# Moving eighteen more exp chunks from ScalarE to VectorE in a fused attention and MLP kernel, with the cost of small jobs reckoned anew

## The chip, the cores and the metric

The kernel runs on one core of one Trainium2 chip. The time is device time in microseconds (us) of one execution; the median of several runs is given, and for every experiment the ratio to the kernel before, timed in the same rounds on the same chip. A ratio is the mean time of one kernel's fast runs over that of the other's of the same rounds, so it is not quite the ratio of the medians that are quoted. Runs of the kernel before lay between 971.1 and 973.6 us in the various rounds; so where two experiments are compared across rounds, their ratios are compared, as a share of 971.5 us.

## The reference, cut to what matters

```python
kv_pool = kv.reshape(B, H//4, 4, W//4, 4, C).mean(axis=(2, 4))     # B 4, C 128, 768 keys per batch
k = v = kv_pool.reshape(B, -1, C) @ w_sr
a = softmax(q @ k.T / sqrt(C))                                     # 49152 queries in all
x = a @ v
h = x @ w_in                                                       # d_ff 2048
out = (h * sigmoid(1.702 * h)) @ w_out
```

The inputs and the output are float32; the kernel computes its matmuls in bf16.

## The kernel before

A *chunk* is 128 keys (or 128 of the d_ff features) by 512 queries. There are 96 groups of 512 queries; four groups make a supergroup. A group needs 6 exp chunks and 16 Gelu chunks. TensorE computes the scores of three chunks into three banks of PSUM (a "fill"), ScalarE takes exp or Gelu of the three in one instruction into a buffer `ag` of 102 slots, and TensorE later multiplies each slot by the values or by `w_out` (a "drain"). So that ScalarE changes its table only three times, the work runs in four stages: attention of the first half, its MoE (the MLP), attention of the second half, its MoE. I call them attention 0, MoE 0, attention 1 and MoE 1.

VectorE already makes the exp of 24 *early* chunks during MoE 0, with a polynomial of ten instructions:

```python
def early_fill(i, jc):
    ps = acc()
    rhs = qTs[i // 4][:, 0, (i % 4) * G:(i % 4 + 1) * G]
    nc.tensor.matmul(ps, kTs[i // GB][:, jc * 128:(jc + 1) * 128], rhs, start=True, stop=True)
    steps = early_exp(ps, weights(("a", i, jc)))
...
def early_exp(ps, out):
    nc.vector.tensor_scalar(a, ps, scale / LN2, -126.0, MUL, MAX)
    yield 3.5
    nc.vector.tensor_scalar(b, a, 127.0, MAGIC, MIN, ADD)
    yield 2.2
    ...
```

The program is written in a fixed order per engine, and the order comes from a reckoning made while it is written: `now` is TensorE's time and `dve` VectorE's, in units of one 512-column matmul (0.2158 us), and `end` is when each activation would end. A drain is placed between two fills when, by the reckoning, its inputs are ready and the next fill is still in time. Nothing of this reckoning happens on the chip. There, TensorE takes its matmuls in the order written, and waits where an input is late (the section on the result shows a wait of 9.11 us in which the matmuls behind it stand still too).

```python
    FIXED, CHUNK, SWITCH, HANDOVER, EVACUATE, LATE = 0.33, 1.975, 6.0, 1.0, 4.5, 1.0
    COST = {pool_chunk: (2.5, 2.0), key_chunk: (0.7, 2.0), ...}
...
        end.append(begin + FIXED + CHUNK * len(part))
```

The transposed queries of a supergroup, `qT`, are loaded by a DMA from supergroup 4 on (before that TensorE transposes them). The load for supergroup s + 2 is issued when ScalarE's fills reach s.

The softmax here doesn't subtract the row's maximum and nothing guards it: scores larger than these inputs give would overflow.

## Time and profile before

972.39 us (median of 3, 972.28 to 972.58); the profiled execution has a span of 969.7 us.

| | busy us | share of the span |
|---|---|---|
| TensorE matmul (PE) | 946.0 | 98% |
| ScalarE (ACT) | 946.4 | 98% |
| VectorE (DVE) | 344.0 | 35% |
| GpSimd (POOL) | 65.7 | 7% |

In the groups, "x512" is the number of instructions, then come busy time and the mean length of one in ns, then the idle time of the engine just ahead of them and what ended it. TensorE's busy time is no measure of its fullness; the prediction shows how its work was counted in its place. The chain of waits of before is shared by ScalarE and TensorE (the page's part on the chain that ended last, by engine and by line):

```profile
ACT 48%; PE 47%; DMA 3%; DVE 1%; issue 1%; POOL 0%; POOLq 0%
```

### The profile page before, as it was taken

The numbers are of one execution on the slowest core, as the hardware profiler recorded it, in microseconds if no ns is written. First come the engines' busy times: TensorE is split into PE (matmuls) and PEld (weight loads), VectorE is DVE, ScalarE is ACT, GpSimd is POOL, SyncE is SP. The second block draws the span as 40 slices with busy tenths as digits, with TensorE's granted clock in tenths as the row PEclk, the third lists the DMA queues.
The fourth block names the chain that finished last, engine by engine and source line by source line (L and its number), as shares of the span: only waits on it lengthen the run. The fifth ranks groups of instructions, "written<-read, shape, count | busy, mean of one in ns | idle before, by whom it ended". The sixth has DMA issues, their size and how long they took to land.

```text
span 969.7 us, 15127 instructions
## 1 busy us (share of the span) xinstructions
PE 946.0 (98%) x6244; PEld 504.7 (52%) x6359; DVE 344.0 (35%) x734; ACT 946.4 (98%) x705; POOL 65.7 (7%) x113
## 2 busy tenths in 40 slices
PE   7899999999999999999999999999999999999997
PEld 3567777544444444454445777754444444444443
DVE  4444433201477778777602333311111011011010
ACT  4999999999999999999999999999999999999997
POOL 3100100340000232000000000000000000000000
PEclk9999999999999999999999999999999999999999
DMA  9899841999862698224348994652222222222222
GB/s 182 161 201 148 110 96 34 108 147 172 162 130 44 103 149 110 41 34 76 57 81 132 182 174 106 131 120 40 37 44 39 38 44 34 43 34 40 37 33 43
DMA packets 354164, 89.66 MB, mean 92 GB/s; under 512 B 328048, under 2 KB 351728, under 8 KB 353776
## 3 DMA queue, kind: packets, MB, share of 16 engines
q1 hardware_dynamic: 323936, 56.06, 33.7%
q0 software_dynamic: 29104, 32.51, 22.6%
q8 instruction: 49, 0.80, 0.3%
q10 hardware_dynamic: 1056, 0.13, 0.1%
q14 instruction: 19, 0.16, 0.1%
HBM read 52.49 MB, written 45.88 MB: 101 GB/s over the span
## 4 chain that ended last, share of the span: by engine, by line
ACT 48%; PE 47%; DMA 3%; DVE 1%; issue 1%; POOL 0%; POOLq 0%
ACT ag L515 36%; PE banks L513 17%; PE banks L520 17%; ACT ag L336 13%; PE banks L345 6%; PE banks L334 5%; DMA qT<-q_bf 2%; DMA x<-in_q_dram 1%; DVE qT L230 1%; PE banks L382 1%; PE banks L424 0%; PE banks L224 0%; DVE o_sb L528 0%; ACT L515 0%; PE banks L134 0%
## 5 line engine op out<-in xcount | busy, mean ns | idle before, releaser
L515 ACT ACTIVATE ag<-banks 128x1536 bf16<-128x1536 f32 x512 | 690.0, 1543 | 1.6 <-PE banks L513 1.5
L513 PE MATMUL banks<-x,w_in_sb 128*128 128x512 bf16 x1484 | 411.2, 379 | 2.9
L520 PE MATMUL banks<-ag,w_out_sb 128*128 128x512 bf16 x1517 | 410.0, 379 | 1.8 <-ACT ag L515 0.5
L336 ACT ACTIVATE ag<-banks 128x1536 bf16<-128x1536 f32 (+1 forms) x188 | 250.6, 1445 | 12.2 <-PE banks L334 11.7
L520 PEld LDWEIGHTS <-w_out_sb 128*128 128x128 bf16 x1536 | 149.6, 97 | 181.7 <-issue 1.6
L513 PEld LDWEIGHTS <-w_in_sb 128*128 128x128 bf16 x1536 | 147.6, 97 | 176.5 <-issue 20.1
L528 DVE STREAM_TRANSPOSE o_sb<-banks 128x512 f32<-128x512 f32 x96 | 68.7, 716 | 398.8 <-PE banks L520 386.5
L345 PEld LDWEIGHTS <-ag 128*128 128x128 bf16 x2304 | 146.4, 98 | 45.4 <-issue 1.2
L345 PE MATMUL banks<-v,ag 128*128 128x129 bf16 x2304 | 162.9, 220 | 0.4 <-DVE v L158 0.3
L334 PE MATMUL banks<-qT,kT 128*128 128x512 bf16 x508 | 146.9, 379 | 9.3 <-ACT ag L336 4.8
L354 DVE RECIPROCAL rec<-banks 128x3 f32<-128x3 f32 x128 | 23.0, 180 | 132.9 <-PE banks L345 132.7
L409 DVE SCALAR_TENSOR_TENSOR ea<-ea,eb 128x512 f32<-128x512 f32 x96 | 65.9, 687 | 2.8
L334 PEld LDWEIGHTS <-kT 128*128 128x128 bf16 x552 | 47.4, 98 | 36.2 <-issue 4.5
L362 DVE TENSOR_TENSOR x<-banks,rec 128x384 bf16<-128x384 f32 x104 | 57.9, 557 | 3.6
L166 POOL DMA_DIRECT2D kvs<-in_kv_dram x32 | 40.4, 1319 | 15.8 <-DMA kvs<-in_kv_dram 11.6
L449 POOL MEMSET gate_tile<- 1x8 f32 x38 | 4.0, 106 | 461.9 <-DVE gate_tile L448 461.9
L398 DVE TENSOR_SCALAR ea<-banks 128x512 f32<-128x512 f32 x24 | 16.6, 691 | 30.1 <-PE banks L382 30.1
L411 DVE SCALAR_TENSOR_TENSOR ag<-ea,ee 128x512 bf16<-128x512 f32 x24 | 16.5, 686 | 1.0
L404 DVE SCALAR_TENSOR_TENSOR eb<-eb,ea 128x512 f32<-128x512 f32 x24 | 16.5, 688 | 0.7
L362 DVE TENSOR_TENSOR xt<-banks,rec 128x384 bf16<-128x384 f32 x24 | 13.4, 557 | 0.8
L230 DVE COPY qT<-banks 128x512 bf16<-128x512 bf16 x15 | 9.8, 686 | 4.8 <-PE banks L224 4.6
L426 DVE COPY x<-banks 128x768 bf16<-128x768 bf16 x12 | 6.7, 557 | 12.0 <-PE banks L424 11.9
(65 smaller groups left out, 154.5 us busy)
## 6 DMA issues: line engine op xcount, KB each, us to landing
out_dram<-o_sb SPq DMA_DIRECT2D x382, 64.0 KB, 2.0
kvs<-in_kv_dram POOLq DMA_DIRECT2D x32, 384.0 KB, 6.2
q_bf<-in_q_dram POOLq DMA_DIRECT2D x20, 512.0 KB, 7.3
x_bf<-x SPq DMA_DIRECT2D x13, 768.0 KB, 5.7
x<-in_kv_dram POOLq DMA_DIRECT2D x12, 512.0 KB, 12.3
x<-in_q_dram POOLq DMA_DIRECT2D x3, 512.0 KB, 20.6
w_in_sb<-in_moe_w_in_dram POOLq DMA_DIRECT2D x1, 512.0 KB, 5.1
w_out_sb<-in_moe_w_out_dram POOLq DMA_DIRECT2D x1, 512.0 KB, 6.6
```

What stands on the lines that cost most here:

```text
L166: nc.gpsimd.dma_start(out=kv_sums[b][:, i2], in_=kv_p[b, i, w, :, i2], **({"accum_op": ADD} if n else {}))
L230: nc.vector.tensor_copy(dst, src)
L334: nc.tensor.matmul(ps[:, k, :], kTs[i // GB][:, jc * 128:(jc + 1) * 128], rhs, start=True, stop=True)
L336: nc.scalar.activation(place([("a",) + c for c in chunks]), ps, AF.Exp, scale=scale)
L345: nc.tensor.matmul(av_of[u][:, k * (C + 1):(k + 1) * (C + 1)], weights(("a", i, jc))[:, o:o + T], vs[i // GB][:, jc, 0:C + 1], start=(jc = ...
L354: nc.vector.reciprocal(rec, ps[:, :, C])
L362: nc.vector.tensor_tensor(to, ps[:, :, 0:C], rec.unsqueeze(2).broadcast_to([128, TS, C]), MUL)
L409: nc.vector.scalar_tensor_tensor(a, a, COEFFS[k], b, ADD, MUL)
L513: nc.tensor.matmul(ps[:, k, :], w_in_sb[:, fc * 128:(fc + 1) * 128], x[:, g % (4 * XS) * G:(g % (4 * XS) + 1) * G], start=True, stop=True)
L515: nc.scalar.activation(place([("m",) + c for c in chunks]), ps, AF.Gelu_apprx_sigmoid)
L520: nc.tensor.matmul(o_of[g], w_out_sb[:, fc, :], weights(("m", g, fc)), start=(fc == 0), stop=(fc == FCH - 1))
L528: nc.vector.transpose(o_sb, o_of.pop(g))
```

## The change

The intent: ScalarE is full, VectorE is not. So one chunk of every supergroup, the last one, goes to VectorE within both attentions too: supergroups 5 to 11 and 13 to 23, 18 chunks. Their results lie in a ring of three slots, `aside`. A chunk's matmul may be placed when the fills have reached the supergroup before its own. And the small jobs of TensorE and the activation are reckoned at their measured length. The diff, cut to its core:

```diff
+    rolling = [(4 * s + 3, JC - 1) for s in range(NS) if 4 * s > early[-1] or QS < s < XS]
+    aside = agpool.tile([128, K, 512], BF, name="aside")
...
+    def early_fits(p, i, jc):
+        if (i, jc) in rolling:
+            group = seq[p][1][0][0] if seq[p][0] == "a" else ...
+            return (i // GB, jc) in vs and i // 4 - 1 <= group // 4 and len(used) > rolling.index((i, jc)) - K
+        return low and min(slot_of.values()) >= low and (2, JC - 1) in vs
+    def early_waits(t):
+        return any(made.get((t // 4, jc), 1e9 if (t // 4, jc) in early_todo else 0.0) > now for jc in range(JC))
...
-    FIXED, CHUNK, SWITCH, HANDOVER, EVACUATE, LATE = 0.33, 1.975, 6.0, 1.0, 4.5, 1.0
-    COST = {pool_chunk: (2.5, 2.0), key_chunk: (0.7, 2.0), value_chunk: (0.7, 2.0),
-            transpose_q: (1.2, 4.0), early_fill: (1.0, 5.5), key_and_value: (1.0, 3.0),
-            transpose_pooled: (1.5, 3.0), make_k: (1.0, 3.0), make_v: (1.5, 3.0), turn: (1.5, 3.5)}
+    FIXED, CHUNK, SWITCH, HANDOVER, EVACUATE, LATE = 0.295, 1.978, 6.0, 1.0, 4.5, 1.0
+    COST = {pool_chunk: (1.9, 2.6), key_chunk: (0.3, 2.4), value_chunk: (0.3, 2.4),
+            transpose_q: (1.05, 4.2), early_fill: (1.0, 5.5), key_and_value: (0.55, 3.5),
+            transpose_pooled: (0.9, 3.6), make_k: (0.8, 3.2), make_v: (0.8, 3.7), turn: (1.55, 3.5)}
```

Cut: two constants made smaller to free SBUF, and the bookkeeping of `made`, `used` and `vs`.

More of the change, by code (lines that the diff above doesn't have):

```diff
@@ L149, in value_chunk @@
         nc.vector.tensor_copy(vs[b][:, jc, 0:C], ps[:, 0:128])
+        vs[b, jc] = True
     def key_and_value(b, jc):
@@ L158, in key_and_value @@
         nc.vector.tensor_copy(vs[b][:, jc, 0:C], ps[:, 128:256])
+        vs[b, jc] = True
     def add_kv(b, n):
@@ L194, in make_v @@
         nc.vector.tensor_copy(vs[b][:, a * K:(a + 1) * K, 0:C], ps[:, :h].rearrange("p (k c) -> p k c", k=K))
-        vs[b, a] = True
+        for jc in range(a * K, a * K + K):
+            vs[b, jc] = True
     qTs = {}
@@ L230, in transpose_q @@
             nc.vector.tensor_copy(dst, src)
-    w_sr_f = cpool.tile([128, C], F32)
+    w_sr_f = npool.tile([128, 512], F32, name="ea", bufs=1)[:, 0:C]
     nc.sync.dma_start(out=w_sr_f, in_=w_sr)
@@ L277 @@
     ag = agpool.tile([128, AG, 512], BF, name="ag")
-    wide = cpool.tile([128, 16, 32], F32R)
-    nc.vector.tensor_copy(wide, ones.unsqueeze(1).broadcast_to([128, 16, 32]))
+    wide = cpool.tile([128, 128], F32R)
+    nc.vector.tensor_copy(wide.rearrange("p (a b) -> p a b", b=32), ones.unsqueeze(1).broadcast_to([128, 4, 32]))
     def warm_wide(n):
         for _ in range(n):
-            nc.tensor.matmul(banks[:, 2, :], wide[:, 0:4, :].rearrange("p a b -> p (a b)"), wide, start=True, stop=True)
+            nc.tensor.matmul(banks[:, 2, :], wide, wide.unsqueeze(1).broadcast_to([128, 4, 128]), start=True, stop=True)
     warm(8)
@@ L325, in weights @@
             return ag[:, (c[1] - early[0]) * JC + c[2], :]
+        if c[0] == "a" and c[1:] in rolling:
+            return aside[:, rolling.index(c[1:]) % K, :]
         return ag[:, slot_of[c], :]
@@ L346, in drain_attn @@
                              vs[i // GB][:, jc, 0:C + 1], start=(jc == 0), stop=(jc == JC - 1))
-            if t % 4 == 3 and i not in early:
+            if t % 4 == 3 and (i, jc) in rolling:
+                used.append((i, jc))
+            elif t % 4 == 3 and i not in early:
                 del slot_of["a", i, jc]
@@ L390, in early_step @@
             steps = None
-            made.add(early_todo.pop(0))
+            made[early_todo.pop(0)] = dve
     def early_exp(ps, out):
@@ L413, in early_exp @@
         yield 3.5
-    made = set()
-    steps, early_todo = None, [(i, jc) for i in early for jc in range(JC)]
+    made, used = {}, []
+    steps, early_todo = None, [c for c in rolling if c[0] < early[0]]
+    early_todo += [(i, jc) for i in early for jc in range(JC)]
+    early_todo += [c for c in rolling if c[0] > early[-1]]
+    def early_fits(p, i, jc):
+        if (i, jc) in rolling:
+            group = seq[p][1][0][0] if seq[p][0] == "a" else seq[p][1][0][0] // (NG // R) * (NG // R) + NG // R - 1
+            return (i // GB, jc) in vs and i // 4 - 1 <= group // 4 and len(used) > rolling.index((i, jc)) - K
+        return low and min(slot_of.values()) >= low and (2, JC - 1) in vs
+    def early_waits(t):
+        return any(made.get((t // 4, jc), 1e9 if (t // 4, jc) in early_todo else 0.0) > now for jc in range(JC))
     def turn(w):
@@ L539 @@
     chunks += [(i, jc) for jc in range(2, JC) for i in range(8)]
-    chunks += [(i, jc) for i in range(8, NG) for jc in range(JC) if i not in early]
+    chunks += [(i, jc) for i in range(8, NG) for jc in range(JC) if i not in early and (i, jc) not in rolling]
     seq, todo = [], []
@@ L562 @@
             at["a", i, jc] = at["a", early[-1] + 1, 0] - 1
+    for i, jc in rolling:
+        at["a", i, jc] = at["a", i, 0]
     for kind, t, a in [k for k in todo + todo_early if k[0] == "a"]:
@@ L651 @@
                 early_step()
-            if not f and not steps and early_todo and low and min(slot_of.values()) >= low and (2, 1) in vs and dve <= now + 2.0 and now >= bank:
+            if not f and not steps and early_todo and early_fits(min(n + 2, len(seq) - 1), *early_todo[0]) and dve <= now + 2.0 and now >= bank:
                 f, args = early_fill, early_todo[0]
@@ L670 @@
             if not source:
-                if todo_early and all((i, jc) in made for t in range(todo_early[0][1], todo_early[0][1] + TS)
-                                      for i in [t // 4] for jc in range(JC)):
+                if todo_early and not any(early_waits(t) for t in range(todo_early[0][1], todo_early[0][1] + TS)):
                     source = todo_early
@@ L683 @@
             if source is not todo_early and (needs > n or (kind == "a" and first_of and at["at", i + TS - 1, 1] > n)
-                                             or (kind == "a" and i // 4 in early and (i // 4, JC - 1) not in made)):
+                                             or (kind == "a" and (early_waits(i) or first_of and early_waits(i + TS - 1)))):
                 if first_of:
```

## The prediction

> **What bounds the kernel now.** I read the engine totals first, then the costliest groups, then ScalarE's timeline, then TensorE cut into windows of 10 and 20 us. From the page of before:
>
> ```profile
> PE 946.0 (98%) x6244; PEld 504.7 (52%) x6359; DVE 344.0 (35%) x734; ACT 946.4 (98%) x705; POOL 65.7 (7%) x113
> ...
> L515 ACT ACTIVATE ag<-banks 128x1536 bf16<-128x1536 f32 x512 | 690.0, 1543 | 1.6 <-PE banks L513 1.5
> ...
> L336 ACT ACTIVATE ag<-banks 128x1536 bf16<-128x1536 f32 (+1 forms) x188 | 250.6, 1445 | 12.2 <-PE banks L334 11.7
> ```
>
> TensorE and ScalarE both show 98%. ScalarE's 946.4 us is honest work: 512 activations of three Gelu chunks and 188 of exp chunks. Its timeline shows how little it waits:
>
> ```profile
> 39.01 32.73 ACT L336 ACTIVATE ag<-banks 128x1536 bf16<-128x1536 f32 x24 [1.44 <-PE banks L334]
> 72.73 76.31 ACT L336 ACTIVATE ag<-banks 128x1536 bf16<-128x1536 f32 x56 [1.00 <-PE banks L334]
> 149.07 1.28 ACT L515 ACT_TABLE_LOAD   x1
> 150.36 274.91 ACT L515 ACTIVATE ag<-banks 128x1536 bf16<-128x1536 f32 x204
> ...
> 428.25 68.80 ACT L515 ACTIVATE ag<-banks 128x1536 bf16<-128x1536 f32 x51 [1.30 <-PE banks L513]
> 497.07 1.28 ACT L336 ACT_TABLE_LOAD   x1
> 498.37 119.23 ACT L336 ACTIVATE ag<-banks 128x1536 bf16<-128x1536 f32 x88
> 617.61 1.28 ACT L515 ACT_TABLE_LOAD   x1
> 618.90 344.90 ACT L515 ACTIVATE ag<-banks 128x1536 bf16<-128x1536 f32 x256
> ```
>
> So there are four stages: attention 0 (to 149), MoE 0 (to 497), attention 1 (to 618), MoE 1 (to 964). After 40 us ScalarE stands still only some 2.5 us in all (1.00 at 72.7 us, 0.23 and 1.30 around 425 us). ScalarE sets the end. Its unit prices follow: 344.90 / 256 = 1.347 us for three Gelu chunks, 119.23 / 88 = 1.355 us for three exp chunks.
>
> How near is TensorE? Its busy column does not say. I counted weight loads per window (one per matmul) and used the spacing of packed matmuls: in the chain of waits three 512-column matmuls take 0.65 us, so 0.216 each; 18 of the 129-column ones take 1.02 us, so 0.057 each. The windows of the second MoE matmul's line (columns: stretch, length, PE busy and count, PEld busy and count, clock, DMA share, GB/s):
>
> ```profile
> 640.00:660.00 20.00, 12.99 (x49) 4.79 (x49) 1.00 0.69 131
> ...
> 800.00:820.00 20.00, 12.69 (x49) 4.59 (x47) 1.00 0.26 40
> 820.00:840.00 20.00, 11.57 (x44) 4.35 (x45) 1.00 0.25 39
> 840.00:860.00 20.00, 11.78 (x45) 4.32 (x45) 1.00 0.21 32
> ```
>
> Until about 817 us TensorE does 48 to 49 of these per 20 us, beside some 45 fills: it is full and working off what it owes. From there it does 45, in lockstep with ScalarE (20 / 1.347 x 3 = 44.5). That is TensorE's whole reserve: from 817 to 963 us it has 146 / 1.347 = 108 activations, in each of which six matmuls take 6 x 0.2158 = 1.295 of 1.347 us; 0.052 x 108 = **5.7 us**. The list of waits agrees:
>
> ```profile
> PEld L513 <- issue: 20.1, 117, 0.3
> ```
>
> 117 waits of 0.17 us for a weight load that finds the queue full; 117 x 0.052 = 6.1 us. So the reserve is about 6 us. Between 80 and 817 us the counts times these prices give 9.8 to 10.4 us per 10 us, no gap.
>
> **What the Trainium skill says.** "Perfetto Trace Analysis", Identifying the Most-Contended Engine: occupancy is a fair measure for ScalarE and VectorE, but matmul busy is none for TensorE. The trace agrees: TensorE's windows show 19.9 of 20 us both before and after 817 us, though it is short of work in one of them. "TensorE: Matmul & The Clock Gate", Back-to-back issue gap: an isolated gap of N/2.4 + 2.5 ns, 215.8 ns for 512 and 56.3 ns for 129 columns; the trace has 216 and 57. The same section's 131 ns for 512 columns in a stream is not what this trace shows. "ScalarE: Activation LUTs", What ACT_TABLE_LOAD costs: 186 ns + 0.833 ns per element for an ACTIVATE with immediates, and an overlap of about 93 ns between two; that makes 1373 ns, and the trace shows 1347 to 1355. So one column of 512 costs some 427 ns of it and cannot be had cheaper. "VectorE: DVE Perf Modes", the perf-mode tier table: fp32 tensor_scalar runs at 2x from SBUF, two-tensor operations and PSUM sources at 1x. The trace: 424 to 438 ns against 686 to 691 ns for 512 elements.
>
> **The change part by part.** (1) Eighteen exp chunks leave ScalarE: `4 < s < 12` gives 7 supergroups in attention 0, `s` of 13 to 23 gives 11 in attention 1. 18 / 3 = 6 activations of 1.355 = **8.1 us** (3.2 in attention 0, 5.0 in attention 1).
>
> (2) VectorE gets 18 more exp polynomials. The rows of before:
>
> ```profile
> L409 DVE SCALAR_TENSOR_TENSOR ea<-ea,eb 128x512 f32<-128x512 f32 x96 | 65.9, 687 | 2.8
> ...
> L398 DVE TENSOR_SCALAR ea<-banks 128x512 f32<-128x512 f32 x24 | 16.6, 691 | 30.1 <-PE banks L382 30.1
> L404 DVE SCALAR_TENSOR_TENSOR eb<-eb,ea 128x512 f32<-128x512 f32 x24 | 16.5, 688 | 0.7
> L411 DVE SCALAR_TENSOR_TENSOR ag<-ea,ee 128x512 bf16<-128x512 f32 x24 | 16.5, 686 | 1.0
> L406 DVE TENSOR_SCALAR ea<-eb 128x512 f32<-128x512 f32 x24 | 10.5, 438 | 0.7
> L402 DVE TENSOR_SCALAR ee<-eb 128x512 int32<-128x512 f32 x24 | 10.2, 426 | 0.7
> L400 DVE TENSOR_SCALAR eb<-ea 128x512 f32<-128x512 f32 x24 | 10.2, 424 | 0.6
> ```
>
> 4 x 687 + 691 + 688 + 686 + 438 + 426 + 424 = 6.1 us each, 110 us in all: VectorE goes from 344 to about 454 us. Inside attention a supergroup on TensorE is 24 x (0.216 + 4 x 0.057) = 10.7 us, and VectorE already spends 16/3 x (0.18 + 0.557) = 3.9 us in it for the normalisation; with 6.1 it has 10.0 of 10.7, so 94%. It fits, barely. Three buffers (`aside`) let it run up to three supergroups ahead of the value matmuls, which lag anyway, and the program only places the value matmuls once it reckons the chunk done. By its own figures (31 units a chunk, 4.3 a normalisation) VectorE needs 54 units a supergroup against TensorE's 49, so in attention 1 the lead shrinks by about 5 x 11 = 55 units, 12 us; the lead is three chunks of 6.7 us. I charge 0 to 1 us of waits.
>
> (3) TensorE's work stays: the same 18 matmuls are issued singly. It loses reserve, because ScalarE ends 8.1 us sooner and TensorE had about 6.
>
> (4) The reckoned costs of small jobs fall (pool_chunk 2.5 to 1.9 units, key_chunk 0.7 to 0.3, and so on; summed over the calls some 23 units, 5 us). Where TensorE is thought busier than it is, too few value matmuls are placed and it waits. From 60 to 80 us the counts make only 17.8 of 20 us; 1.2 of the gap is a wait for a qT load. I estimate that 0.5 to 1.5 us of TensorE time come back. Against that the activation is now reckoned at 0.295 + 3 x 1.978 = 6.229 units, 1.344 us, just under the measured 1.347 and 1.355: TensorE may get a little too little work while it owes some, 0.003 x 400 + 0.011 x 180 = 3 us at most, partly swallowed by the double buffer. I take these two as cancelling.
>
> (5) The smaller `wide` and the shared w_sr_f only make room in SBUF: zero.
>
> Sum: ScalarE alone would give 972.4 - 8.1 = 964.3; TensorE alone allows 972.4 - 6 = 966.4, give or take the terms of (4). The later one wins: **966.3 us**.
>
> **Rivals.** *ScalarE stays the bound, all 8.1 us arrive:* 964. For it speaks part (4) if it frees 2 us. *The buffer of weights fills:* TensorE owes a lot when attention 0 ends (275 value-matmul weight loads from 150 to 180 us, 69 chunks), and by fills minus drains some 57 to 67 chunks wait through MoE 0, where only 102 - 24 = 78 slots may be used. With ScalarE 3.2 us earlier up to 15 more would wait: the buffer is full, ScalarE stands still 1.5 to 3 us in MoE 0, and attention 0's gain is lost there. This mostly coincides with TensorE's bound; on top of it, 968. *VectorE becomes the bound inside attention:* value matmuls wait for late chunks, TensorE idles 3 to 6 us it cannot make up: 970 to 972. The 94% speaks for it, the lead of three chunks against. *Late qT loads:* ScalarE is faster from supergroup 5 on, while the queues are at 0.9 to 1.1 of their share until 130 us; only one such wait (1.2 us) is seen before, so a small risk, 968.
>
> **Range and chances.** No path leads to 953, since ScalarE would then have to give up 19 us of work: faster 0.01. Over 992 would need a broken schedule: 0.02. The range takes the full 8.1 us plus a little retuning at the low end and VectorE's waits at the high end: 963.3 to 970.5.
>
> **What would show it.** Right: 18 more of each polynomial row (72 more of the L409 kind), VectorE near 454 us, exp activations 6 fewer, ScalarE near 938 us busy; the lockstep at the end of MoE 1 gone or down to a few activations; ScalarE idle 1 to 3 us in MoE 0. Wrong: value matmuls waiting for VectorE in attention for more than 2 us (then slower), or lockstep still lasting 50 us or more before the end (then TensorE found reserve that I didn't see, and the time is near 964).

## The result, and the profile after

982.61 us (median of 4, 981.16 to 983.02) against 972.49 us of before in the same rounds; ratio 1.0099 (1.0082 to 1.0117). The change made the kernel about 10 us slower, and the prediction of 966.3 us, with a range to 970.5, was wrong.

Most of what I forecast of the engines came true; of the exceptions, the exp activations are 5 fewer and not 6 (188 to 183), and ScalarE stands still 5.2 us in MoE 0, where I had said 1 to 3. The engine totals, the chain's shares and two groups of the page after (columns as before):

```profile
PE 953.1 (97%) x6359; PEld 508.6 (52%) x6359; DVE 444.5 (45%) x914; ACT 936.9 (95%) x700; POOL 65.7 (7%) x113
...
PE 82%; ACT 13%; DMA 3%; DVE 1%; issue 0%; POOL 0%; POOLq 0%
...
L343 ACT ACTIVATE ag<-banks 128x1536 bf16<-128x1536 f32 (+1 forms) x183 | 241.5, 1496 | 22.0 <-PE banks L341 21.9
...
L418 DVE SCALAR_TENSOR_TENSOR ea<-ea,eb 128x512 f32<-128x512 f32 x168 | 115.2, 686 | 3.8
```

ScalarE works 9.5 us less, VectorE 100 us more, L418 (the L409 of before) has the 72 more instructions. But the span grew by 11.6 us, and the chain is now TensorE's. ScalarE's idle time ahead of the exp activations rose from 12.2 to 22.0 us. Its timeline after shows where (start, length, engine, line, instruction, count, and the idle time before):

```profile
38.78 24.43 ACT L343 ACTIVATE ag<-banks 128x1536 bf16<-128x1536 f32 x18 [1.43 <-PE banks L341]
72.96 1.45 ACT L343 ACTIVATE ag<-banks 128x1536 bf16<-128x1536 f32 x1 [9.75 <-PE banks L341]
...
664.00 305.14 ACT L535 ACTIVATE ag<-banks 128x1536 bf16<-128x1536 f32 x227 [0.96 <-PE banks L533]
```

At 63 us ScalarE stops for 9.75 us. TensorE's timeline of that moment tells why:

```profile
61.30 0.56 PE L134 MATMUL banks<-sum,x 128*128 128x32 bf16 x16
...
70.97 0.61 PE L391 MATMUL banks<-qT,kT 128*128 128x512 bf16 x1 [9.11 <-DMA qT<-q_bf]
...
71.37 1.49 PE L341 MATMUL banks<-qT,kT 128*128 128x512 bf16 x3
```

L391 is the score matmul of a chunk set aside, that of supergroup 5. It was placed while the fills were still in supergroup 4. The load of that qT was issued at 48.06 us, just after six loads of kv of 512 KB each (3.2 us of issuing from 44.60 us on), and landed 22.9 us later, at 70.96; the median of all twenty loads of qT is 6.5 us. (That the kv loads are what delayed it is read from this order; no run moved them.) Nobody else needed it before about 71 us. But one matmul that came too soon held up everything behind it in TensorE's order. When it went on, its clock had dropped; the matmuls at 71 to 74 us take twice their usual spacing, and the granted clock from 70.0 to 76.5 us is 0.50. The wait and, by estimate, some 2.5 to 3 us lost at half the clock make up the 11.6 us of this stretch in the table below.

For the whole span I counted TensorE's work again as in the prediction: weight loads per window of 20 us, by line, times the spacing of packed matmuls (0.2158 us for 512 columns, 0.0567 for 129, and estimates for the few small ones). What is left of a window is TensorE's idle time. Summed over stretches, in us:

```text
                 0-40   40-80  80-480  480-660  660-960   sum    span   span - sum
before           12.1    1.9    -0.6    -0.7      4.1     16.8   969.7    952.9
after            12.0   11.6    -0.7     5.8     -0.7     28.0   981.3    953.3
```

The negative entries show the error of the method, a few tenths of a per cent. The last column is a check of the counting and no proof: both kernels run the same number of matmuls, and idle time was defined as what their work leaves of a window, so the span less the idle time must come out alike (953 us of matmuls and tail), whatever sets the pace. What the table finds is *where* the idle time lies. The difference of 11.2 us in the sum has three parts: +9.7 for the qT, +6.5 around the end of attention 1, and -4.8 at the end, which is the reserve that the prediction found (the lockstep is gone, as it said).

The second part looks quite different on TensorE's and VectorE's timelines after. Here all that TensorE does from 644.3 to 647.4 us is three fills (L533), two of which wait for ScalarE to free their banks:

```profile
644.86 0.68 DVE L420 SCALAR_TENSOR_TENSOR aside<-ea,ee 128x512 bf16<-128x512 f32 x1
...
645.59 0.81 PE L533 MATMUL banks<-x,w_in_sb 128*128 128x512 bf16 x3 [0.54 <-ACT ag L535]
...
646.93 0.81 PE L533 MATMUL banks<-x,w_in_sb 128*128 128x512 bf16 x3 [0.54 <-ACT ag L535]
...
648.36 0.10 PEld L352 LDWEIGHTS <-aside 128*128 128x128 bf16 x1
```

The chunk is done at 645.5 us; its first value matmul comes at 648.4. TensorE doesn't wait for the chunk: no wait of a value matmul for a chunk's last step is in the list. The drains are simply not there in the order, since the program reckoned the chunk would be done later than it was (the fifth experiment tests this).

### The profile page after: what moved, and what is told of

Same layout as the page of the kernel before. It is cut to its first block, busy times and chain, and to the rows that moved or that the text cites. A ratio compares the mean times of both kernels' runs of the same rounds, so it can differ in the third digit from the quotient of the medians.

```text
span 981.3 us, 15454 instructions
## 1 busy us (share of the span) xinstructions
PE 953.1 (97%) x6359; PEld 508.6 (52%) x6359; DVE 444.5 (45%) x914; ACT 936.9 (95%) x700; POOL 65.7 (7%) x113
## 4 chain that ended last, share of the span: by engine, by line
PE 82%; ACT 13%; DMA 3%; DVE 1%; issue 0%; POOL 0%; POOLq 0%
PE banks L540 34%; PE banks L533 32%; ACT ag L343 9%; PE banks L352 7%; PE banks L341 7%; ACT ag L535 3%; DMA qT<-q_bf 2%; PE banks L391 1%; DMA x<-in_q_dram 1%; DVE qT L233 1%; PE banks L444 0%; DVE xt L371 0%; PE banks L227 0%; PE banks L134 0%; DVE x L446 0%
## 5 line engine op out<-in xcount | busy, mean ns | idle before, releaser
L533 PE MATMUL banks<-x,w_in_sb 128*128 128x512 bf16 x1536 | 415.0, 379 | 4.0 <-ACT ag L535 3.0
L343 ACT ACTIVATE ag<-banks 128x1536 bf16<-128x1536 f32 (+1 forms) x183 | 241.5, 1496 | 22.0 <-PE banks L341 21.9
L533 PEld LDWEIGHTS <-w_in_sb 128*128 128x128 bf16 x1536 | 147.9, 98 | 172.8 <-issue 6.9
L341 PE MATMUL banks<-qT,kT 128*128 128x512 bf16 x534 | 146.5, 382 | 5.6 <-ACT ag L343 4.5
L418 DVE SCALAR_TENSOR_TENSOR ea<-ea,eb 128x512 f32<-128x512 f32 x168 | 115.2, 686 | 3.8
L407 DVE TENSOR_SCALAR ea<-banks 128x512 f32<-128x512 f32 x42 | 29.1, 692 | 60.1 <-PE banks L391 59.9
L363 DVE RECIPROCAL rec<-banks 128x3 f32<-128x3 f32 x128 | 22.9, 179 | 55.2 <-PE banks L352 54.9
L413 DVE SCALAR_TENSOR_TENSOR eb<-eb,ea 128x512 f32<-128x512 f32 x42 | 28.9, 689 | 1.0
L391 PE MATMUL banks<-qT,kT 128*128 128x512 bf16 x42 | 16.1, 384 | 9.1 <-DMA qT<-q_bf 9.1
L415 DVE TENSOR_SCALAR ea<-eb 128x512 f32<-128x512 f32 x42 | 18.2, 434 | 0.9
L411 DVE TENSOR_SCALAR ee<-eb 128x512 int32<-128x512 f32 x42 | 17.9, 427 | 1.3
L409 DVE TENSOR_SCALAR eb<-ea 128x512 f32<-128x512 f32 x42 | 17.8, 423 | 1.0
## 6 DMA issues: line engine op xcount, KB each, us to landing
x<-in_kv_dram POOLq DMA_DIRECT2D x12, 512.0 KB, 12.4
```

The lines of the kernel that those rows point to most:

```text
L341: nc.tensor.matmul(ps[:, k, :], kTs[i // GB][:, jc * 128:(jc + 1) * 128], rhs, start=True, stop=True)
L343: nc.scalar.activation(place([("a",) + c for c in chunks]), ps, AF.Exp, scale=scale)
L413: nc.vector.scalar_tensor_tensor(b, b, MAGIC, a, SUB, SUB)
L418: nc.vector.scalar_tensor_tensor(a, a, COEFFS[k], b, ADD, MUL)
L533: nc.tensor.matmul(ps[:, k, :], w_in_sb[:, fc * 128:(fc + 1) * 128], x[:, g % (4 * XS) * G:(g % (4 * XS) + 1) * G], start=True, stop=True)
```

## The experiments

My theory had two causes: the qT that is not there yet, and value matmuls placed too late. Rivals: the new reckoning of costs alone; real slowness of VectorE; and a buffer of weights that fills. Eleven kernels ran; all gave correct results.

### Costs alone

```diff
-    rolling = [(4 * s + 3, JC - 1) for s in range(NS) if 4 * s > early[-1] or QS < s < XS]
+    rolling = []
```

> The changed kernel with no rolling chunks at all: only the shorter reckoned costs of small jobs and the new handling of early chunks remain. Theory (the chunks cost the time, through a TensorE wait for a qT load and through TensorE idling for late chunks): 971 to 974 us, the wait for qT near 71 us is 1 to 2 us as before, and the lockstep at the end of the second MoE stays. Rival A (the new reckoning orders TensorE's work badly by itself): 977 us or more, with new gaps on TensorE.

968.35 us; ratio 0.9967 (0.9953 to 0.9982). Rival A falls: the reckoning doesn't hurt, it gains about 3.2 us, which I had not expected (I had said the two terms cancel). So on top of the new reckoning the chunks cost some 13 us.

### Chunks alone

```diff
-    FIXED, CHUNK, ... = 0.295, 1.978, ...      COST as changed
+    FIXED, CHUNK, ... = 0.33, 1.975, ...       COST as before
```

> The changed kernel with the reckoned costs of before: only the 18 chunks. Theory: the early matmul of supergroup 5 is still issued one supergroup ahead of its qT, so TensorE waits 7 to 10 us near 62 to 71 us, and the time is 980 to 984 us. Rival A (the reckoning is to blame): no wait over 2 us and 966 to 969 us.

979.4 us; ratio 1.0082, just under the 980 to 984 expected. TensorE's wait for qT is 8.1 us. The stall belongs to the chunks. But the two halves do not add: the chunks alone cost 8.0 us and the reckoning alone gains 3.2, which would make 4.8 us, and both together cost 9.6. The other 4.8 us are not explained in full; in the table below, the idle times of 40 to 80 and of 480 to 660 us are 1.7 and 2.4 us larger with both.

### No chunk ahead of ScalarE in attention 0

```diff
-            ... i // 4 - 1 <= group // 4 and ...
+            ... i // 4 - (i > early[-1]) <= group // 4 and ...
```

> The changed kernel, where in attention 0 a chunk's score matmul may only be placed once ScalarE's own fills have reached that supergroup (in attention 1 still one ahead). Theory: the 9.1 us wait shrinks to the 1 to 2 us of before, TensorE's idle time in attention 1 stays near 5 us, and the time is 972 to 975 us. Rival B (the qT load is late for ScalarE as well, so the wait only moves to its own score matmul): 979 us or more.

973.33 us; ratio 1.0023 against 1.0099, so 7.4 us are back (by the two spans, 971.2 against 981.3, it is 10.1; the profiled run of after was the slowest of its four). The wait that was 9.1 us (the list of waits of this run: who waited for what, us in all, times, longest):

```profile
PE banks L341 <- DMA qT<-q_bf: 1.2, 1, 1.2
```

It is the same load, landing at nearly the same time (71.8 us), and now it costs what it cost before the change. Rival B falls. TensorE's idle time from 480 to 660 us is unchanged, 5.6 us.

### Only the eleven chunks of attention 1

```diff
+    rolling = [(4 * s + 3, JC - 1) for s in range(NS) if 4 * s > early[-1]]
```

> The changed kernel with only the 11 chunks of attention 1. Theory: no wait for qT beyond 2 us; ScalarE has 5.0 us less to do, but TensorE idles some 5 us between 620 and 662 us for chunks that VectorE finishes late, so its reserve of 6 us is gone and the time is 970 to 973 us. Rival C (late chunks cost nothing, as TensorE makes up for it): 967 to 968.5 us.

970.4 us; ratio 0.9991 (0.9976 to 1.0005). No qT wait over 1.4 us, idle time from 480 to 660 us 5.7 us. Against the run with costs alone, eleven chunks that save ScalarE 5 us made the kernel 2.3 us slower. Rival C falls: TensorE makes up for only about 3 of the 6.4 us, its idle time after 660 us (1.9 down to -1.1 in the table below), and then has no reserve left.

### The same, with VectorE's steps reckoned as measured

A run of two steps on two tensors takes 1.41 us (after), of which the last step is 0.69; so 0.72 us from start to start, 3.3 units; the program had 3.5. The one-tensor steps take 0.46 us, 2.1 units; it had 2.2. A normalisation takes 0.18 + 0.56 us, to which I added two gaps of 0.03, 3.7 units; it had 4.3. (In the trace the next step starts 0.68 us after the normalisation did, as at 560.61 and 561.29 us, which is 3.2 units; so 3.7 is still on the long side.)

```diff
-            on_dve(4.3)
+            on_dve(3.7)
...
-        yield 3.5        (all of them; and 2.2 to 2.1)
+        yield 3.3
```

> The 11 chunks of attention 1 only, with VectorE's own steps reckoned near their measured length too (3.3 and 2.1 units for the steps of a chunk in place of 3.5 and 2.2, 3.7 for a normalisation in place of 4.3). So far span = 953.2 us + TensorE's idle time held within 0.5 us for all kernels. Theory (TensorE's 4.3 us of idle time between 480 and 660 us come from the program's reckoning of VectorE, not from VectorE, since no wait of TensorE for a chunk was seen): that idle time falls to 1 us or less, span 963.5 to 965, time 965 to 967 us. Rival D (VectorE really is too slow there): waits of TensorE for the chunk's last step appear, idle time stays at 3 us or more, time 969.5 to 972 us.

964.7 us; ratio 0.9930 (0.9917 to 0.9944). This is the best of all runs, 6.8 us faster than the kernel before. It is even a little better than I expected (965 to 967 us). VectorE has the same instructions to do; only when the program believes them done was changed, and with it the place of each step in the order. TensorE's idle time from 480 to 660 us fell from 5.7 to 0.4 us, and no wait of a value matmul for a chunk came up. Rival D falls. The reckoning does more than hold drains back that could have come: it also paces the chunks themselves. From 559 to 603 us they are done every 14.8 us in the run before this, and every 12.4 us from 554 to 604 us in this one (ScalarE's share of a supergroup is 113.5 / 11 = 10.3 us); the last is done at 646.4 and 630.6 us. ScalarE's timeline in MoE 1 of the run before this (eleven chunks, old reckoning of VectorE), then of this one:

```profile
651.41 305.14 ACT L535 ACTIVATE ag<-banks 128x1536 bf16<-128x1536 f32 x227 [0.96 <-PE banks L533]
```

```profile
612.90 343.14 ACT L535 ACTIVATE ag<-banks 128x1536 bf16<-128x1536 f32 x255 [0.16 <-PE banks L533]
```

ScalarE ends at nearly the same time in both (956.6 and 956.0 us), but the spans are 968.7 and 962.9 us: in the first TensorE still owes 39 drains after its last fill, in the second 15, and 24 drains are 5.2 us. This is where a gain of ScalarE goes that TensorE can't follow.

### Every other supergroup of attention 1

```diff
+    rolling = [(4 * s + 3, JC - 1) for s in range(NS) if 4 * s > early[-1] and s % 2]
```

> 6 chunks in attention 1, one in every other supergroup, none in attention 0, all reckonings as in the changed kernel. Theory: VectorE's reckoned load per supergroup falls from 54 to 38 units, under TensorE's 49, so the late idle time vanishes; ScalarE has 2 activations less (2.7 us), of which TensorE's lockstep idle of 3.2 us covers all: 965 to 967 us. Rival D' (any chunk set aside costs TensorE as much as it saves): 968 to 970 us.

965.26 us; ratio 0.9935 (0.9920 to 0.9950). Six chunks with the old reckoning of VectorE gain nearly as much as eleven with the new one: the reckoned load fits, and TensorE's idle time from 480 to 660 us is 0.0. Rival D' falls.

### The activation's reckoning alone

No rolling chunks, `COST` as before, `FIXED, CHUNK` as in the change.

> No rolling chunks, small jobs reckoned as before the change, only the activation reckoned as in the change (0.295 + 3 x 1.978). Theory (the 3 us that the costs alone gained come from the activation's reckoning, since the activations' spacing in the second MoE fell from 1.347 to 1.344 us): 968 to 969.5 us, spacing 1.344 to 1.345 us. Rival E (the small jobs' reckoning gave it, by filling gaps on TensorE in attention 0): 971 to 973 us, spacing 1.347 us.

970.65 us; ratio 0.9993 (0.9978 to 1.0008). Both predictions of time missed on one side or the other: the spacing is 344.21 / 256 = 1.3446 us as the theory said, but the time hardly moved. ScalarE stands still 0.36 + 1.30 + 0.18 us in MoE 0 here, where the run with both reckonings has only 0.37 us.

### The small jobs' reckoning alone

No rolling chunks, `COST` as in the change, `FIXED, CHUNK` as before.

> No rolling chunks, the small jobs reckoned as in the change, the activation as before the change: the complement of the run that changed only the activation's reckoning (0.9 us gained). Both together gained 3.1 us. Theory (the two gains simply add, the small jobs give the rest by filling TensorE between 60 and 80 us): 969 to 970 us, activation spacing in the second MoE 1.347 us. Rival (each is worth something only with the other): 971 us or more.

970.92 us; ratio 0.9993 (0.9981 to 1.0006), between the two ranges expected. Here the standstill in MoE 0 is 0.30 us, but the spacing is 345.00 / 256 = 1.3477 us. So the two gains don't add; the 3.2 us of both together come only with both. The numbers fit this: with both, ScalarE's spacing is lower by 0.003 to 0.010 us in some 680 activations (2.4 us), and it stands still 0.7 us less after 40 us. That the one undoes the other's standstill through a fuller buffer of weights is argued here; the last table of this section speaks for it.

### All eighteen, nothing ahead, VectorE reckoned as measured

The edits of the third and fifth experiment together.

> All 18 chunks, with no chunk placed ahead of ScalarE in attention 0, and VectorE's steps reckoned near their measured length. Theory: idle time in attention 1 as in the run with 11 chunks (1 us or less), attention 0 with at most 1 us more than that run; 965 to 968 us, so faster than the kernel before by 4 to 6 us. Rival F (the seven chunks of attention 0 bring nothing, as TensorE is full and the buffer of weights stops ScalarE in the first MoE): within 0.7 us of the run with 11 chunks or slower, with ScalarE idle 2 to 5 us in the first MoE.

969.27 us; ratio 0.9978 (0.9963 to 0.9993), a miss against 965 to 968. Faster than before by 2.1 us, but 4.7 us slower than the same with eleven chunks. Rival F is right about that. Its two parts: TensorE gets some 2.7 us more idle time between 80 and 160 us than with eleven chunks; and in MoE 0 ScalarE stands still for TensorE:

```profile
415.25 83.73 ACT L535 ACTIVATE ag<-banks 128x1536 bf16<-128x1536 f32 x62 [2.59 <-PE banks L533]
```

In total 6.1 us in that stage (before: 1.5; with eleven chunks 0.7). So what ScalarE is spared in attention 0 is handed back twice over within MoE 0: this stage starts 2.6 us earlier than with eleven chunks and ends 3.9 us later.

### Four chunks of attention 0 added to the best kernel

```diff
+    rolling = [... if 4 * s > early[-1] or 7 < s < XS]
```

> The run with 11 chunks and VectorE's steps reckoned as measured (964.7 us), plus four chunks of attention 0, of supergroups 8 to 11 alone and not ahead of ScalarE. Theory (the seven chunks cost 4.6 us because in supergroups 5 to 7 VectorE also evacuates transposes, and each of its delays is a gap on TensorE, which is full): with the four later ones TensorE's idle time between 80 and 160 us grows by 0.7 us at most, time 964.5 to 966 us. Rival G (any chunk of attention 0 costs some 0.65 us): 967 us or more.

967.33 us; ratio 0.9956 (0.9942 to 0.9969). My theory (that VectorE's evacuations in supergroups 5 to 7 make the cost) falls: four later chunks cost 2.5 us too, 0.6 us each, as rival G said. TensorE's idle time grew by 0.7 us until 160 us and by 2.6 us in all, in portions too small for this counting to place. On ScalarE's timeline the cost is easier to see: it stands still 3.4 us in MoE 0 (0.7 with eleven chunks), 2.47 us of it in one piece that ends at 413.1 us, as in the run before this one; the stage starts 2.0 us earlier and ends 1.8 us later. The two runs that are compared here are on two chips, so only by their ratios.

### Without the chunk of supergroup 5

```diff
+    rolling = [... if 4 * s > early[-1] or QS + 1 < s < XS]
```

> The changed kernel without the chunk of supergroup 5, the other 17 still placed one supergroup ahead. Theory (only the qT of supergroup 5 is late, as its load was issued at 48 us behind six loads of kv of 512 KB each; later qT loads land in time): no wait of TensorE for a qT over 2 us, 972 to 974.5 us. Rival H (placing ahead is the fault, whichever supergroup): the wait moves to supergroup 6 with 4 us or more, 977 us or more.

974.38 us; ratio 1.0028 (1.0016 to 1.0041). The other six chunks of attention 0 are still placed one supergroup ahead, and no wait for a qT exceeds 1.3 us. Rival H falls: it was one chunk, whose matmul met one late load. From 480 to 660 us TensorE idles 6.3 us as before.

TensorE's idle time of all these runs, counted as above (of the fifth and the sixth, 2.5 us of the last stretch lie past TensorE's end and are taken off):

```text
                   40-80  80-480  480-660  660-960    sum    span   span - sum
costs alone          0.9    -1.2    -0.7      1.9     13.2   966.6    953.4
chunks alone         9.9     0.5     3.4     -0.8     25.4   978.6    953.2
none ahead           0.4     1.3     5.6     -1.1     18.4   971.2    952.8
attention 1 only     0.7    -2.3     5.7     -1.1     15.0   968.7    953.7
 + VectorE reckoned  0.5    -2.0     0.4     -1.2      9.9   962.9    953.0
every other          0.8    -1.7     0.0     -1.9      9.2   963.6    954.4
all, none ahead      0.6     1.7     1.7     -2.2     13.7   967.4    953.7
last four added      0.6    -0.2     1.3     -1.2     12.5   965.3    952.8
without five         0.8     2.0     6.3     -1.1     20.1   972.5    952.4
```

(The first 40 us are 11.9 to 12.4 in every run.) Over a spread of 18 us in span, the last column stays within 2 us; as said, this checks the counting and is no finding.

The program's reckoning can be run again without the chip, from the kept kernels: it is plain Python. Counted were the drains in MoE 0 that were placed past the next fill's deadline because at most 9 slots of the buffer of weights were free; by how much the fills came late for it, in us; and how often, after the last fill of attention 1, a drain was held back because its chunk was not yet reckoned done. Beside them stand the measured standstill of ScalarE in MoE 0 and TensorE's idle time from 480 to 660 us:

```text
                    MoE 0: forced   late by   measured    held back for   idle,
                          drains              standstill  a chunk         480-660
before                      14        1.8       1.5            0           -0.7
costs alone                 20        0.6       0.4            0           -0.7
activation alone            46        2.5       1.8            0            -
small jobs alone             6        0.0       0.3            0            -
after                       70        5.4       5.2            9            5.8
chunks alone                60        5.3       4.3            6            3.4
none ahead                  90        4.7       4.4            6            5.6
attention 1 only            20        0.6       0.4            6            5.7
 + VectorE reckoned         14        0.6       0.7            0            0.4
every other                 20        0.6       0.4            0            0.0
all, none ahead             80        6.2       6.1            0            1.7
last four added             67        3.9       3.4            0            1.3
without five                91        5.4       5.3            9            6.3
```

The two costs part cleanly. Drains are held back for a chunk in every run in which TensorE idles 3.4 us or more from 480 to 660 us, and in none that has 1.7 us or less. And ScalarE's standstill in MoE 0 goes with drains that a nearly full buffer forces ahead of a fill; that is what the chunks of attention 0 run into. In the run with all eighteen, TensorE does 36 value matmuls and four matmuls by `w_out` between the fills at 410.08 and 414.35 us, in the trace as in the reckoning. No run tested this by a larger buffer.

## Why the prediction was wrong, point by point

**What bounds the kernel.** Right, and the most useful part: ScalarE sets the pace, TensorE has only some 6 us of reserve, at the end (by the count above 4.8). After the change the lockstep is gone and TensorE is the chain.

**Part (1), ScalarE's saving.** 8.1 us were said, as 6 activations; 5 went, as the chunks that are left do not divide by three in each half, and the partly filled ones are shorter. Its busy time fell by 9.5 us, of which part is the closer spacing.

**Part (2), VectorE's load and waits.** The load was nearly right (444.5 us against 454 said). The step that failed is "I charge 0 to 1 us of waits". I had worked out from the program's own figures that VectorE is reckoned at 54 units a supergroup against TensorE's 49, and took the lead of three chunks to absorb it. It didn't: 5.8 us of TensorE idle time from 480 to 660 us. And the mechanism was neither of those I named, the chunk done in time or TensorE waiting for it: the reckoning, too long for VectorE, spaced the chunks out and held their drains back, so that the order itself lacked them. Reckoning VectorE nearer to its measured length removed 5.3 of those us (fourth against fifth experiment).

**Part (3), "TensorE's work stays: the same 18 matmuls are issued singly".** This step failed most. The work stayed, but I did not ask *when* each matmul is issued against when its operand lands. The rival "Late qT loads" looked at ScalarE's own pace only and was put at 968. The condition `i // 4 - 1 <= group // 4` in the diff, and the 1.2 us wait for the same qT at 72 us in the profile before, held the answer: a load that is just in time for its supergroup is a supergroup's length too late for a matmul placed one ahead. It cost 9.7 us with the slow clock after it, by the profiled runs; taking the early placement away gave 7.4 us back by the ratios.

**Part (4), reckoning.** I took the gain and the loss as cancelling. Measured, the costs alone gain 3.2 us. I called 1.344 us for an activation too low; in the runs that use it the spacing is 1.344 to 1.346 us, and with the old one 1.347 or more, so the 1.347 of before was made by the old reckoning. That it let fills come a little late is argued.

**The sum.** 966.3 said. With TensorE's limit as I had it plus the two idle times, 966.3 + 9.7 + 6.5 = 982.5, against 982.61: the sum was missing these two terms, which together were charged with 0 to 1 us. (That it agrees so closely is luck: part (4) was off by 3 us as well, and the two terms come from the profiled run, the slowest of its four.) By the ratios, taking away the early placement gave 7.4 us and the reckoning of VectorE 4.4 us more (the third experiment, and all eighteen reckoned as measured against it), together more than the 9.6 us lost. What is left is 2.1 us faster than before, not the 6 us forecast; the rest is the next point.

**Rivals.** The full buffer of weights came true, and larger than I put it: ScalarE stands still 3.4 to 6.1 us in MoE 0 in the runs with chunks in attention 0 (5.2 in the changed kernel), where I said 1.5 to 3. I took it to coincide mostly with TensorE's limit; with both other causes gone, the seven chunks of attention 0 still left the kernel 4.7 us slower than without them. Neither sign of being wrong that I had named came: value matmuls waited 0.2 us for VectorE, and no lockstep was left.

## What to carry to other kernels

When work moves off one full engine onto an idle one, ask what the *other* full engine does with it: in these runs eleven chunks less on ScalarE (5 us) made the kernel slower by 2.3 us or faster by 3.6 us, according to whether TensorE's drains were placed late or not (fourth and fifth experiment, against costs alone). An instruction that is moved forward in an engine's order must have its operand landed at the new place, not at the old one. And where a program orders its instructions by reckoned times, measure every engine's entry: reckoning VectorE's work of a supergroup at 54 units where 49 would do cost 5.9 us (fourth against fifth experiment).

## What the Trainium skill lacked or had wrong

- "TensorE: Matmul & The Clock Gate", Back-to-back issue gap, gives sustained stream rates of 131 ns for 512 and about 81 ns for 128 columns. In this kernel, full of pairs of weight load and matmul, the spacing is 216 ns and (129 columns) 57 ns, which are the values that the page gives for the isolated gap.
- "ScalarE: Activation LUTs", What ACT_TABLE_LOAD costs: 186 ns + 0.833 ns per element less about 93 ns of overlap makes 1373 ns for 1536 elements. The trace has 1.45 us for one that stands alone and a closest spacing of 305.14 / 227 = 1.344 us, so the overlap seen here is about 106 ns (122 ns against the page's own length of 1466 ns).
